# Two tiles of the first layer norm transposed by one DMA instead of two, and the transposed tiles laid out tile by tile

## The chip, the core and the metric

The kernel runs on one core of a Trainium2 chip. The time is the device time of one execution in microseconds; three executions of the kernel before gave 169.84, 170.46 and 170.59 us, so its median is 170.46 us. One more execution was profiled; its own time is 170.56 us, and the profile's times count from its first instruction.

Engines are named as in the profile: PE (TensorE matmuls), PEld (TensorE weight loads), DVE (VectorE), ACT (ScalarE), POOL (GpSimd) and SP (SyncE). SP computes nothing here: it issues all DMAs.

## The reference

A transformer block: linear attention on the layer norm of x, and a ReLU network on the layer norm of the result, each with a residual sum. The shapes are S = 2048 rows, D = 512, H = 32 heads of 16, Dff = 1792; everything is bfloat16.

```python
def _A_ref(x, wqkv, wo):
    q, k, v = ...                      # x @ wqkv, split into 32 heads of 16
    pq, pk = phi(q), phi(k)            # phi(t) = where(t > 0, t + 1, exp(t)) + 1e-6
    kv = einsum("bhsd,bhse->bhde", pk, v)
    z = einsum("bhsd->bhd", pk)
    num = einsum("bhqd,bhde->bhqe", pq, kv)
    den = einsum("bhqd,bhd->bhq", pq, z)[..., None] + 1e-6
    return (num / den) ... @ wo

h = x + _A_ref(_layernorm(x), A_wqkv, A_wo)
h2 = h + relu(_layernorm(h) @ w1) @ w2
```

## The kernel before

The 2048 rows are 16 tiles of 128 rows (tile number t, 0 to 15), and four tiles make a chunk of 512 rows (chunk c, 0 to 3). The order of all work is written out by hand in the string `ORDER`: each word names an operation and its numbers, and the words are carried out in that order. Engines run side by side; each engine takes its own instructions in the order of the words. So a word stands for a place in the queue of one engine.

The words that matter here, for a tile t of the first layer norm:

- `S.t` and `A.t` (DVE, L237 and L238) take mean and variance of x; `R.t.n` (ACT, L243 and L244) makes the reciprocal standard deviation of n tiles; `N.t` (DVE, L262) writes the normalised tile into `h_nat`.
- `X.t` (SP, L302) issues a transposing DMA that turns the tile of `h_nat` (128 rows by 512 features) into four blocks of 128 features by 128 rows, in `lnT[c]`. Tiles 0 to 3 go through PE instead (`T.t`, L281) and are copied from PSUM by ACT (`E.t`, L291).
- `K.t.b` (PE, L310) multiplies the transposed tile with the key weights: four matmuls of 512 columns into PSUM bank b, with the blocks of `lnT` as the stationary operand. `F`, `U` (ACT, L328 and L331), `M`, `D` (DVE, L335 and L338) make phi of the result.
- `G.t` (PE, L362) adds the tile's share of the sum over rows of layer norm times pk: four matmuls of 512 columns.
- `Q.c.j.b` (PE, L318) makes the queries of a whole chunk: four matmuls whose moving operand is `lnT[c]`, 512 rows wide.

After the attention, `lnT[c]` is used again for the second layer norm: `x.t` (SP, L303) transposes a tile of it by DMA, and `p.c.f.b` (PE, L521) multiplies a chunk with the first weights of the ReLU network, again with `lnT[c]` as the moving operand; `f` (PE, L541) is the second layer of that network, `fo` (DVE, L549) the last sum, and `fd` (SP, L556) the store.

Chunk 2 holds tiles 8 to 11. Its tiles are transposed in the order 9, 8, 11, 10. In `ORDER`, `N.9` is followed by `S.12`, `X.6`, `N.8`, `X.9`; `X.8` comes a line later. On PE the words stand as `K.7.3 G.1 K.6.2 K.9.1 G.4 K.8.0 G.5 G.6`.

The layout of a transposed chunk and how a tile is found in it:

```python
lnT = [big.tile([P, KD, CW], BF16, name=f"lnT{c}") for c in range(NCH)]   # KD = 4, CW = 512

def lnT_of(t, k=0, n=KD):
    c, j = divmod(t, CT)
    return lnT[c][:, k : k + n, j * P : (j + 1) * P]
```

So each partition of `lnT[c]` holds four feature blocks of 512 rows, and a tile's 128 rows lie in four pieces, one in each block.

Of the kernel before, what the change touches and what calls it, by code (L numbers as in the profile page):

```python
# [11 lines left out]
BF16 = mybir.dt.bfloat16  # L12
# [7 lines left out]
lx.4.2 A.2 T.0.7 E.0 warm.1.3 S.3 R.2.1 K.0.1.0.2 lx.6.2 A.3 R.3.1 K.0.1.2.2 N.1 T.1.5 F.0.1 E.1 N.2 N.3 T.3.2  # L20
lx.8.4 E.3 S.4 S.5 A.4 T.2.5 lx.12.4 lq.0.2 A.5 K.1.0.0.2 R.4.2 S.6 M.0.1 N.5 S.7 N.4 X.5 E.2 U.0.1 D.0.1 K.3.7
K.1.0.2.2 F.3.1 M.3.1 X.4 K.2.3.0.2 U.3.1 A.7 A.6 K.2.3.2.2 U.1.1 R.6.2 F.2.1 F.1.1 G.0 D.3.1 G.3 S.9 U.2.1 N.7
N.6 S.8 K.5.1 K.4.0 M.2.1 A.8 A.9 R.8.2 U.4.2 M.1.1 X.7 D.2.1 F.4.2 D.1.1 N.9 S.12 X.6 N.8 X.9 G.2 K.7.3 S.13
A.12 A.13 G.1 R.12.2 K.6.2 K.9.1 M.4.2 S.10 F.6.2 N.12 D.4.2 S.11 A.10 U.6.2 X.8 M.6.2 N.13 G.4 X.12 K.8.0 A.11
R.10.2 S.14 D.6.2 G.5 G.6 X.13 N.10 N.11 S.15 F.8.2 M.8.2 X.11 A.15 U.8.2 A.14 D.8.2 R.14.2 G.7 za.2 za.4 K.12.0
G.9 K.13.1 N.15 N.14 X.10 lq.2.2 K.11.3 F.12.2 K.10.2 M.12.2 U.12.2 F.10.2 masks X.15 X.14 lv.0.2 lv.2.2 l1.0.2
U.10.2 za.6 D.12.2 M.10.2 G.8 za.8 D.10.2 Q.0.1.1 Q.0.0.0 qF.0.0.2 qU.0.0.2 za.10 G.12 K.14.2 K.15.3 Q.0.2.0
# [29 lines left out]
def kernel(  # L57
# [10 lines left out]
    nc = tc.nc  # L68
    P = 128
    xf = A_x.flatten_outer_dims()  # L70
    of = out.flatten_outer_dims()
    S, D = xf.shape
# [4 lines left out]
    CW = 512  # L77
    CT = CW // P
    NCH = S // CW
    KD = D // P  # L80
# [8 lines left out]
    big = ctx.enter_context(tc.tile_pool(name="big", bufs=1))  # L89
# [12 lines left out]
    wq_sb = const.tile([P, KD, D], BF16, name="wq_sb")  # L102
    wk_sb = const.tile([P, KD, D], BF16, name="wk_sb")
    wv_sb = const.tile([P, KD, D], BF16, name="wv_sb")
    wo_sb = const.tile([P, KD, D], BF16, name="wo_sb")
    w1_sb = const.tile([P, KD, FF], BF16, name="w1_sb")
# [8 lines left out]

    h_nat = big.tile([P, NT, D], BF16, name="h_nat")
    ln_nat = h_nat
    lnT = [big.tile([P, KD, CW], BF16, name=f"lnT{c}") for c in range(NCH)]
    pqT = [big.tile([P, KD, CW], BF16, name=f"pqT{c}") for c in range(NCH)]
    gT = big.tile([P, KD, D], BF16, name="gT")  # L120
    kvbd = big.tile([P, KD, P], BF16, name="kvbd")
# [23 lines left out]
    bk = psum.tile([P, 8, CW], F32, name="bk")  # L145
# [127 lines left out]

    def lnT_of(t, k=0, n=KD):
        c, j = divmod(t, CT)
        return lnT[c][:, k : k + n, j * P : (j + 1) * P]

    def transpose(src, b, k, n):
        tp = bank16(b, n)
# [10 lines left out]
    def op_E(t, k=0, n=KD):  # L290
        nc.scalar.activation(out=lnT_of(t, k, n), in_=at_bank["T", t, k], func=ACT.Copy)  # L291

    def op_V(t, k=0, n=KD):
        nc.vector.tensor_copy(out=lnT_of(t, k, n), in_=at_bank["T", t, k])

    def op_e(t):
        nc.scalar.activation(out=lnT_of(t), in_=at_bank["t", t, 0], func=ACT.Copy)
# [4 lines left out]
    op_X = lambda t: nc.sync.dma_start_transpose(out=lnT_of(t), in_=ln_nat[:, t, :])  # L302
    op_x = lambda t: nc.sync.dma_start_transpose(out=lnT_of(t), in_=hn[:, t % NQ, :])  # L303


    def op_K(t, b, k=0, n=KD):
        c, j = divmod(t, CT)
        at_bank["k", t] = b
        for kd in range(k, k + n):
            nc.tensor.matmul(  # L310
                bk[:, b, :], lhsT=lnT[c][:, kd, j * P : (j + 1) * P], rhs=wk_sb[:, kd, :],
                start=(kd == 0), stop=(kd == KD - 1),
            )

    def op_Q(c, j, b):
        at_bank["q", c * KD + j] = b
        for kd in range(KD):
            nc.tensor.matmul(  # L318
                bk[:, b, :], lhsT=wq_sb[:, kd, j * P : (j + 1) * P], rhs=lnT[c][:, kd, :],
                start=(kd == 0), stop=(kd == KD - 1),  # L320
            )

# [194 lines left out]
    def op_p(c, f, b, s=0, n=1):  # L517
        at_bank["p", c, f] = b
        cols = slice(s * CW // n, (s + 1) * CW // n)
        for kd in range(KD):  # L520
            nc.tensor.matmul(  # L521
                bk[:, b, cols], lhsT=w1_sb[:, kd, f * P : (f + 1) * P], rhs=lnT[c][:, kd, cols],
                start=(kd == 0), stop=(kd == KD - 1),
            )

# [66 lines left out]
```

## Time and profile before

| | |
|---|---|
| three runs | 169.84, 170.46, 170.59 us |
| the profiled execution's own time | 170.56 us |
| its span, first to last instruction | 168.8 us |
| PE busy | 163.1 us, 855 matmuls recorded |
| DVE busy | 104.4 us |
| ACT busy | 65.1 us |
| DMA, share of 16 engines | 35.5% |

Between the profiled execution's own time and its span lie 1.8 us that no row of the trace shows. The page of the profile gives busy times, the chain of work that ended last (each step followed back to what released it), and the groups of instructions with what ended the idle time before them. Further views: the timeline of one engine in a stretch, in which neighbouring instructions of one kind are merged ("x4" are four of them, and the microseconds are from the first start to the last end); the DMA view, which lists issues with their median time from issue to landing; and the table of stretches, whose columns are the length, then for each engine its busy time and number of instructions, the granted clock of TensorE (1.00 is full speed), the mean busy share of the 16 DMA engines and the rate in GB/s. Matmul records overlap: a matmul's row is its latency, so the time that each takes in a row of equal ones is read from the distance between starts. Some matmul records are missing from the trace.

### The profile page before, as it was taken

Reading aid. Unit: us, or ns where it says so; the run is one execution under the profiler, and the core shown is the slowest. Engines: PE = TensorE matmul, PEld = TensorE weight load, DVE = VectorE, ACT = ScalarE, POOL = GpSimd, SP = SyncE. Lnnn points to the kernel's source line nnn. Section 1 sums busy time; section 2 is a strip of 40 time slices with the busy share of each in tenths; the row PEclk is TensorE's granted clock in tenths of the full one; section 3 lists DMA queues with packets and bytes.
Section 4 is the critical chain, followed back from the end, with each engine's and each line's share of the span. In section 5 each row is a group of like instructions: output and inputs, shape, how many; then the busy total and the mean of one; then the engine's idle time right before and its main releaser. Section 6 shows DMA issues by size and latency. Waiting matters only on the chain.

```text
span 168.8 us, 2286 instructions
## 1 busy us (share of the span) xinstructions
PE 163.1 (97%) x855; PEld 78.0 (46%) x871; DVE 104.4 (62%) x205; ACT 65.1 (39%) x97; POOL 4.8 (3%) x21
## 2 busy tenths in 40 slices
PE   7989999999999999999999999999999999999993
PEld 5344344445644454444444444444444444444553
DVE  3899998997668999699819879215102432050251
ACT  3698775875879947432000003004320420400000
POOL 7400000000000000000000000000000000000000
PEclk9999999999999999999999999999999999999999
DMA  4975575689533353534130015500320000002023
GB/s 112 352 245 97 97 66 124 176 270 378 174 64 65 77 138 87 134 62 95 37 62 0 31 31 122 126 4 0 62 93 0 31 0 4 0 0 93 0 65 94
DMA packets 30491, 15.49 MB, mean 92 GB/s; under 512 B 23184, under 2 KB 29328, under 8 KB 30480
## 3 DMA queue, kind: packets, MB, share of 16 engines
q1 hardware_dynamic: 30480, 15.34, 35.5%
q8 instruction: 7, 0.11, 0.3%
q14 instruction: 4, 0.03, 0.1%
HBM read 7.86 MB, written 2.10 MB: 59 GB/s over the span
## 4 chain that ended last, share of the span: by engine, by line
PE 85%; DVE 7%; DMA 4%; issue 1%; SPq 0%
PE bk L541 29%; PE bk L521 28%; PE bk L505 8%; PE bk L318 8%; PE bk L362 6%; PE bk L310 4%; DVE st L237 3%; DMA x_nat<-in_A_x_dram 2%; DMA lnT<-h_nat 2%; DVE h_nat L262 2%; PE bk L459 1%; DVE eb L335 1%; PE bk L403 1%; PE bk L415 1%; SPq L201 0%
## 5 line engine op out<-in xcount | busy, mean ns | idle before, releaser
L541 PE MATMUL bk<-w_sb,at 128*128 128x512 bf16 (+2 forms) x247 | 50.1, 355 | 0.3
L521 PE MATMUL bk<-lnT,w_sb 128*128 128x512 bf16 x219 | 50.0, 379 | 0.3
L527 ACT ACTIVATE at<-bk 128x1024 bf16<-128x1024 f32 x14 | 14.2, 1023 | 57.4 <-PE bk L521 57.4
L541 PEld LDWEIGHTS <-at 128*128 128x128 bf16 x252 | 23.6, 98 | 25.4 <-ACT at L527 0.3
L549 DVE SCALAR_TENSOR_TENSOR gT<-bk,rstd,h_nat 128x512 bf16<-128x512 f32 (+2 forms) x18 | 12.2, 689 | 35.7 <-PE bk L541 35.6
L521 PEld LDWEIGHTS <-w_sb 128*128 128x128 bf16 x224 | 21.8, 98 | 25.8
L532 DVE TENSOR_SCALAR at<-bk 128x1024 bf16<-128x1024 f32 x14 | 17.1, 1218 | 12.8 <-PE bk L521 12.6
L328 ACT ACTIVATE eb<-bk 128x1024 bf16<-128x1024 f32 (+1 forms) x18 | 16.6, 928 | 6.6 <-PE bk L310 4.8
L310 PE MATMUL bk<-wk_sb,lnT 128*128 128x512 bf16 x63 | 15.3, 380 | 0.4 <-ACT lnT L291 0.3
L505 PE MATMUL bk<-m_sb,pqs 128*128 128x512 bf16 x63 | 15.4, 380 | 0.1
L318 PE MATMUL bk<-lnT,wq_sb 128*128 128x512 bf16 x61 | 15.1, 379 | 0.1
L362 PE MATMUL bk<-at,h_nat 128*128 128x512 bf16 x55 | 13.5, 379 | 0.1
L331 ACT ACTIVATE rb<-bk 128x1024 bf16<-128x1024 f32 (+1 forms) x14 | 12.5, 904 | 0.3 <-PE bk L310 0.3
L511 DVE TENSOR_TENSOR h_nat<-bk,x_nat 128x512 bf16<-128x512 f32 x16 | 10.5, 680 | 2.9 <-PE bk L505 2.9
L237 DVE BATCH_NORM_STATS2 st<-x_nat 128x6 f32<-128x512 bf16 x16 | 10.8, 680 | 2.4 <-DMA x_nat<-in_A_x_dram 2.4
L239 DVE BATCH_NORM_STATS2 st<-h_nat 128x6 f32<-128x512 bf16 x16 | 10.7, 683 | 0.1
L310 PEld LDWEIGHTS <-lnT 128*128 128x128 bf16 x64 | 6.0, 98 | 8.4 <-ACT lnT L291 1.0
L362 PEld LDWEIGHTS <-h_nat 128*128 128x128 bf16 x64 | 6.2, 98 | 7.4 <-issue 0.2
L505 PEld LDWEIGHTS <-pqs 128*128 128x128 bf16 x64 | 5.9, 98 | 7.9 <-DVE pqs L495 1.8
L318 PEld LDWEIGHTS <-wq_sb 128*128 128x128 bf16 x64 | 5.9, 98 | 6.4
L472 ACT ACTIVATE wk_sb<-ld 128x1024 bf16<-128x1024 f32 x8 | 8.1, 1050 | 0.1
L335 DVE TENSOR_SCALAR eb<-eb 128x1024 bf16<-128x1024 bf16 (+1 forms) x18 | 6.8, 383 | 0.9 <-ACT eb L328 0.9
(63 smaller groups left out, 93.5 us busy)
## 6 DMA issues: line engine op xcount, KB each, us to landing
out_dram<-gT SPq DMA_DIRECT2D x15, 128.0 KB, 1.9
w_sb<-in_B_w_dram SPq DMA_DIRECT2D x2, 896.0 KB, 9.8
x_nat<-in_A_x_dram SPq DMA_DIRECT2D x2, 512.0 KB, 6.3
w_sb<-in_B_w_dram SPq DMA_DIRECT2D x2, 512.0 KB, 9.5
x_nat<-in_A_x_dram SPq DMA_DIRECT2D x3, 256.0 KB, 4.6
w_sb<-in_B_w_dram SPq DMA_DIRECT2D x2, 384.0 KB, 3.5
wk_sb<-in_A_wqkv_dram SPq DMA_DIRECT2D x2, 256.0 KB, 4.3
wq_sb<-in_A_wqkv_dram SPq DMA_DIRECT2D x2, 256.0 KB, 4.9
```

What stands on the lines that cost most here:

```text
L237: op_S = lambda t: nc.vector.bn_stats(out=st[:, t, :], in_=x_nat[:, t, :])
L310: nc.tensor.matmul(bk[:, b, :], lhsT=lnT[c][:, kd, j * P : (j + 1) * P], rhs=wk_sb[:, kd, :], start=(kd == 0), stop=(kd == KD - 1),)
L318: nc.tensor.matmul(bk[:, b, :], lhsT=wq_sb[:, kd, j * P : (j + 1) * P], rhs=lnT[c][:, kd, :], start=(kd == 0), stop=(kd == KD - 1),)
L328: nc.scalar.activation(out=buf(eb, kind, i, n), in_=bank(at_bank[kind, i], n), func=ACT.Exp)
L331: nc.scalar.activation(out=buf(rb, kind, i, n), in_=bank(at_bank[kind, i], n), func=ACT.Relu)
L362: nc.tensor.matmul(bk[:, KD + kd, :], lhsT=ln_nat[:, t, kd * P : (kd + 1) * P], rhs=pk(t)[:, 0, :], start=(t == 0), stop=(t == NT - 1),)
L505: nc.tensor.matmul(bk[:, b, :], lhsT=pqs[:, (c * KD + jb) % NQ, j * P : (j + 1) * P], rhs=m_sb[:, jb, :], start=(jb == 0), stop=(jb == KD ...
L521: nc.tensor.matmul(bk[:, b, cols], lhsT=w1_sb[:, kd, f * P : (f + 1) * P], rhs=lnT[c][:, kd, cols], start=(kd == 0), stop=(kd == KD - 1),)
L527: nc.scalar.activation(out=acts[c % 2][:, f : f + n, :], in_=bank(at_bank["p", c, f], n), func=ACT.Relu)
L532: nc.vector.tensor_scalar(out=acts[c % 2][:, f : f + n, :], in0=bank(at_bank["p", c, f], n), scalar1=0.0, scalar2=None, op0=ALU.max,)
L541: nc.tensor.matmul(bk[:, b, 0 : w * P], lhsT=acts[c % 2][:, f, j * P : (j + 1) * P], rhs=w2_sb[:, f, k * P : (k + w) * P], start=(f == 0), ...
L549: nc.vector.scalar_tensor_tensor(out=o_t[:, t % NO, cols], in0=bk[:, at_bank["f", t, k], 0 : w * P], scalar=rstd2[:, t : t + 1], in1=h_nat ...
```

## The change

Three things change.

1. `lnT[c]` is laid out tile by tile: first the tile in the chunk, then its feature block, then 128 rows. A tile's four blocks now lie side by side (512 elements of a partition). The four feature blocks of one tile are next to each other, and the 512 rows of one feature block, which the moving operand of `Q` and `p` reads, lie in four pieces of 128, 512 elements apart.
2. A new operation `XX.t` issues one transposing DMA for tiles t and t + 1: 128 rows by 1024 columns in, eight blocks out. `XX.8` stands where `X.9` stood, and `X.8` is gone.
3. `N.8` moves ahead of `S.12` and `X.6`, directly behind `N.9`.

```diff
-N.6 S.8 K.5.1 K.4.0 M.2.1 A.8 A.9 R.8.2 U.4.2 M.1.1 X.7 D.2.1 F.4.2 D.1.1 N.9 S.12 X.6 N.8 X.9 G.2 K.7.3 S.13
-A.12 A.13 G.1 R.12.2 K.6.2 K.9.1 M.4.2 S.10 F.6.2 N.12 D.4.2 S.11 A.10 U.6.2 X.8 M.6.2 N.13 G.4 X.12 K.8.0 A.11
+N.6 S.8 K.5.1 K.4.0 M.2.1 A.8 A.9 R.8.2 U.4.2 M.1.1 X.7 D.2.1 F.4.2 D.1.1 N.9 N.8 S.12 X.6 XX.8 G.2 K.7.3 S.13
+A.12 A.13 G.1 R.12.2 K.6.2 K.9.1 M.4.2 S.10 F.6.2 N.12 D.4.2 S.11 A.10 U.6.2 M.6.2 N.13 G.4 X.12 K.8.0 A.11
...
-    lnT = [big.tile([P, KD, CW], BF16, name=f"lnT{c}") for c in range(NCH)]
+    lnT = [big.tile([P, CT, KD, P], BF16, name=f"lnT{c}") for c in range(NCH)]
...
-        return lnT[c][:, k : k + n, j * P : (j + 1) * P]
+        return lnT[c][:, j, k : k + n, :]
...
+    def op_XX(t):
+        c, j = divmod(t, CT)
+        nc.sync.dma_start_transpose(
+            out=lnT[c][:, j : j + 2].rearrange("p t k n -> p (t k) n"),
+            in_=ln_nat[:, t : t + 2, :].rearrange("p t d -> p (t d)"),
+        )
...
-                bk[:, b, :], lhsT=lnT[c][:, kd, j * P : (j + 1) * P], rhs=wk_sb[:, kd, :],
+                bk[:, b, :], lhsT=lnT[c][:, j, kd, :], rhs=wk_sb[:, kd, :],
...
-                bk[:, b, :], lhsT=wq_sb[:, kd, j * P : (j + 1) * P], rhs=lnT[c][:, kd, :],
+                bk[:, b, :], lhsT=wq_sb[:, kd, j * P : (j + 1) * P], rhs=lnT[c][:, :, kd, :],
...
-                bk[:, b, cols], lhsT=w1_sb[:, kd, f * P : (f + 1) * P], rhs=lnT[c][:, kd, cols],
+                bk[:, b, cols], lhsT=w1_sb[:, kd, f * P : (f + 1) * P], rhs=lnT[c][:, s * CT // n : (s + 1) * CT // n, kd, :],
```

How the order of instructions moves, at two places. First DVE, around the normalising of tiles 9 and 8 (`h_nat` is where the normalised tiles go, `st` the statistics; the first L262 below is tile 9, the second tile 8, and the two L237 are the statistics of tiles 12 and 13). Before:

```order
L338 TENSOR_TENSOR at_94<-rb,eb 128x512
L338 TENSOR_TENSOR pk_lo<-rb,eb 128x512
L262 TENSOR_SCALAR h_nat<-x_nat,mv,rstd 128x512
L237 BN_STATS st<-x_nat 128x6
L262 TENSOR_SCALAR h_nat<-x_nat,mv,rstd 128x512
L237 BN_STATS st<-x_nat 128x6
L238 BN_AGGR mv<-st 128x2 x2
```

And with the change:

```order
L345 TENSOR_TENSOR at_94<-rb,eb 128x512
L345 TENSOR_TENSOR pk_lo<-rb,eb 128x512
L262 TENSOR_SCALAR h_nat<-x_nat,mv,rstd 128x512 x2
L237 BN_STATS st<-x_nat 128x6 x2
L238 BN_AGGR mv<-st 128x2 x2
```

Tile 8 is normalised directly behind tile 9, one statistics instruction earlier than before; that statistics instruction is one normalisation later, and from the second one on the order is as it was.

Second SP's queue of DMAs, from the first load of the query weights to the second (`lnT_82`, `lnT_83` and `lnT_84` are the chunks 1, 2 and 3). Before:

```order
L204 DMA wq_sb<-in_A_wqkv_dram 128x2x512
L302 DMA_TRANSPOSE lnT_82<-h_nat 128x4x128 x4
L302 DMA_TRANSPOSE lnT_83<-h_nat 128x4x128 x2
L302 DMA_TRANSPOSE lnT_84<-h_nat 128x4x128 x2
L302 DMA_TRANSPOSE lnT_83<-h_nat 128x4x128 x2
L204 DMA wq_sb<-in_A_wqkv_dram 128x2x512
```

And with the change:

```order
L204 DMA wq_sb<-in_A_wqkv_dram 128x2x512
L302 DMA_TRANSPOSE lnT_82<-h_nat 128x4x128 x4
L307 DMA_TRANSPOSE lnT_83<-h_nat 128x8x128
L302 DMA_TRANSPOSE lnT_84<-h_nat 128x4x128 x2
L302 DMA_TRANSPOSE lnT_83<-h_nat 128x4x128 x2
L204 DMA wq_sb<-in_A_wqkv_dram 128x2x512
```

The fifth and sixth transposing DMA, of tiles 9 and 8, are one; all others keep their place and size. PE's instructions keep their order.

## The prediction

> **What bounds the kernel now.** I read the page's shares first, then the chain of work that ended last, then the stretch around tiles 8 and 9.
>
> ```profile
> PE 163.1 (97%) x855; PEld 78.0 (46%) x871; DVE 104.4 (62%) x205; ACT 65.1 (39%) x97; POOL 4.8 (3%) x21
> PE 85%; DVE 7%; DMA 4%; issue 1%; SPq 0%
> ```
>
> PE is busy 97% of the span. The chain of waits (start, length, what) says from when on it alone sets the end:
>
> ```profile
> 16.77 0.31 DVE h_nat L262
> 17.09 0.57 DVE st L237
> 17.65 3.40 DMA lnT<-h_nat
> 21.05 0.04 issue
> 21.10 1.04 PE bk L310 x4
> 22.14 2.59 PE bk L362 x12
> ...
> 166.16 0.03 issue
> 166.18 0.35 DVE gT L549
> ```
>
> From 21.10 to 166.16 every step of the chain is PE or a gap of some 0.05 us. The step before is a transposing DMA of 3.40 us, issued at 17.65: that of tile 8, for which `K.8` waits. So what the change does to the moment at which PE gets through `K.8` goes to the end nearly in full, both ways. Changes on DVE, ACT or SP count only through this.
>
> The stretch itself, from the timelines of SP, PE, PEld and DVE:
>
> ```profile
> 15.04 1.22 SPq L302 DMA_TRANSPOSE lnT<-h_nat  x1
> 16.34 1.22 SPq L302 DMA_TRANSPOSE lnT<-h_nat  x1
> 17.65 1.22 SPq L302 DMA_TRANSPOSE lnT<-h_nat  x1
> 19.16 1.19 SPq L302 DMA_TRANSPOSE lnT<-h_nat  x1
> 18.21 1.89 PE L310 MATMUL bk<-wk_sb,lnT 128*128 128x512 bf16 x8
> 19.94 1.03 PE L362 MATMUL bk<-at,h_nat 128*128 128x512 bf16 x4
> 21.09 0.55 PEld L310 LDWEIGHTS <-lnT 128*128 128x128 bf16 x4 [0.63 <-DMA lnT<-h_nat]
> 15.76 0.41 DVE L262 TENSOR_SCALAR h_nat<-x_nat,mv,rstd 128x512 bf16<-128x512 bf16 x1
> 16.09 0.69 DVE L237 BATCH_NORM_STATS2 st<-x_nat 128x6 f32<-128x512 bf16 x1
> 16.69 0.40 DVE L262 TENSOR_SCALAR h_nat<-x_nat,mv,rstd 128x512 bf16<-128x512 bf16 x1
> 18.74 0.40 DVE L262 TENSOR_SCALAR h_nat<-x_nat,mv,rstd 128x512 bf16<-128x512 bf16 x1
> ```
>
> The SP rows are `X.6`, `X.9`, `X.8` and `X.12`. The eight matmuls from 18.21 are `K.6` and `K.9`. Eight take 1.73 us from start to start (19.94 − 18.21), 0.216 each, so `K.9` starts at 19.07. The four of `G.4` end their turn at 19.94 + 0.86 = 20.80. `K.8` starts at 21.10: PE stands still for 0.30 us there. `K.9` did not wait; `X.9` landed in time.
>
> Why `X.8` took 3.40 us, where others take 2.5:
>
> ```profile
> DMA to landing us min/median/max: 2.4/2.5/4.1
> q14 instruction: 1, 0.01, 8.5%
> ```
>
> The second row is the DMA view of the stretch 19.4 to 19.8: one instruction fetch lay on the DMA engines just as this transfer ended. That is an inference from the coincidence; it explains the extra 0.9 us.
>
> **The change part by part.**
>
> *The pair's issue.* `N.9` ends at 15.76 + 0.41 = 16.17. `N.8` now follows it instead of the statistics. Neighbouring normalisation and statistics start 0.33 apart (15.76 to 16.09), so `N.8` ends at 16.50. SP is through with `X.6` at 16.26. `X.12` was issued 0.02 behind its normalisation (18.74 + 0.40, then 19.16). So `XX.8` is issued at 16.5, against 16.34 for `X.9` and 17.65 for `X.8`.
>
> *Its landing* is the term that decides, and no row shows a transposing DMA of this size. What one tile's transfer consists of is seen in stretches of DMA activity:
>
> ```profile
> 17.40:17.60 0.20, 0.20 (x3) 0.08 (x2) 0.20 (x1) 0.20 (x1) 0.00 (x0) 1.00 0.14 23
> 17.60:18.20 0.60, 0.60 (x4) 0.26 (x3) 0.60 (x5) 0.42 (x2) 0.00 (x0) 1.00 1.02 202
> 18.20:18.40 0.20, 0.20 (x2) 0.10 (x1) 0.20 (x2) 0.17 (x2) 0.00 (x0) 1.00 0.19 28
> 18.40:18.80 0.40, 0.40 (x3) 0.20 (x2) 0.40 (x2) 0.07 (x1) 0.00 (x0) 1.00 0.00 0
> ```
>
> `X.9`, issued at 16.34, moves its data from about 17.55 to 18.3: 1.2 us until the data start, 0.75 us of data with the DMA engines full (share 1.02), and 0.5 us until the landing, 2.45 in all. Bounds for twice the data:
>
> - Low: it lands like one tile, after 2.4 us (the least landing time), at 18.9. `K.9` does not wait, and `K.8` finds its data there: PE gains the 0.30 us.
> - High: the issue doubles to 2.45, data begin only at its end, as they now begin when the issue of 1.22 ends, and take 1.5, then the 0.5: 4.45 us, at 20.95. `K.9` starts at 20.99, 1.92 late; less the 0.30 that `K.8` no longer waits, PE loses 1.62.
> - By the distance of two issues (17.65 − 16.34 = 1.31) instead of the data: 2.45 + 1.31 = 3.76, at 20.26, PE loses 20.30 − 19.07 − 0.30 = 0.93.
> - By the data alone: 2.45 + 0.75 = 3.2, at 19.7, PE loses 0.37.
>
> Which is nearest? A plain store of 128 KB:
>
> ```profile
> 92.54 0.36 SPq L556 DMA_DIRECT2D out_dram<-gT  x1
> 92.90:93.30 0.40, 0.40 (x4) 0.20 (x2) 0.28 (x1) 0.00 (x0) 0.00 (x0) 1.00 0.00 0
> 93.30:93.50 0.20, 0.20 (x3) 0.10 (x1) 0.00 (x0) 0.00 (x0) 0.00 (x0) 1.00 0.33 108
> ```
>
> Its issue ends at 92.90 and its data start after 93.30, at least 0.4 behind. A transposing DMA's data start when its issue ends, so they seem to stem from an early part of the issue, and a longer issue would overlap its data. I take the data bound with a little for the issue: 3.25 us, landing at 16.5 + 3.25 = 19.75.
>
> [...]
>
> *PE.* `K.9` starts at 19.79 (0.04 behind the landing, as after 21.05) in place of 19.07: +0.72. `G.4` follows at once, and `K.8`, whose tile lies in the same DMA, does not wait: −0.30. Sum **+0.42 us**. Queued behind the waiting `K.9` on PE are `G.4`, `K.8` and everything else, so the loss stays; DVE and ACT, which wait for `K.8`'s sums, only wait longer.
>
> *What is moved past.* The statistics of tile 12 start 0.33 later, those of tile 13 as before, so `N.12` (18.74) and `X.12` (19.16) stay; SP is free before: 16.5 + 2.45 at most is 18.95. One issue of about 1.2 is saved if the pair costs no more than one, on a queue that no later chain step shows: 0.
>
> *The layout.* ACT's copies into `lnT` wrote four pieces of 128 and now write 512 in a row; the rows show no cost of pieces to get back, since a copy into a plain row takes as long:
>
> ```profile
> L291 ACT ACTIVATE lnT<-bk x4: 579/594/604, 6.3 to 10.2; 128x512 bf16<-128x512 bf16 x4
> 14.01 0.60 ACT L331 ACTIVATE rb<-bk 128x512 bf16<-128x512 f32 x1
> ```
>
> The other transposing DMAs write contiguous rows now; PE waits for two of L302 at most (1.0 us of weight loads in all), of L303 never. So 0, while that cover holds. `K`'s weight loads still read 128 neighbours. But 64 matmuls of `Q` and 224 of `p` now read the moving operand in four pieces. No matmul of before does. Below: nothing. Above: each piece costs what a matmul of 128 columns costs by itself:
>
> ```profile
> 42.79 0.89 PE bk L403 x16
> 29.91 1.73 PE bk L318 x8
> ```
>
> 0.89 / 16 = 55.6 ns, times four 222.5, against 1.73 / 8 = 216.3 ns: 6.2 ns on 288 matmuls, 1.8 us. I take 0: a matmul of 512 columns already streams for 216 ns without a break that depends on where its columns lie, and the separate matmuls pay for a start of their own, which one instruction has not.
>
> Sum: 170.56 + 0.42 = 170.98 for the profiled execution, which lies 0.10 above the median of the runs: **170.9 us** against 170.46.
>
> **The rivals.**
>
> 1. *The pair lands like one tile* (low bound): PE gains 0.30, 170.2 us. For it: the granularity of an issue could be the instruction. Against it: the DMA engines are full (share 1.02) during one tile's 0.75 us, so twice the data needs more time, unless the contiguous destination moves faster. [...]
> 2. *The pair lands 4 us or more after its issue*, since data wait for the whole issue, or since they meet the fetch at 19.5, which cost `X.8` 0.9 us: 3.25 + 0.9 puts the landing at 20.65, PE loses 1.32; with the high bound 1.62. 171.8 to 172.1 us. For it: the fetch came at 19.5 and may come again, as DVE, ACT and SP reach that moment unchanged. Against it: the pair's data run from 17.7 to 19.2, just ahead. It decides as soon as the landing passes 20.2 (over 0.85 lost).
> 3. *The moving operand in pieces costs time*: 1.8 us on top of 0.42, 172.7 us; from 1.5 ns a matmul (0.43 us) on it carries the sum past 0.5%. For it: no row excludes it. Against it: above.
>
> **How the numbers follow.** Forecast 0.53, rival 1 0.07, rival 2 0.25, rival 3 0.12, and 0.03 for a gain that I cannot name. A measurement of this kernel tells about 0.5%, 0.85 us, from no change: 169.6 to 171.3. The forecast's own range is 170.6 to 171.3 (landing after 3.0 to 3.7 us); I give a tenth of it to beyond 171.3. Slower: 0.25 + 0.12 + 0.05 = 0.42. Faster: 0.03, since rival 1 gains only 0.2%. Within: 0.55. The range reaches from rival 1 to rival 2, 170.1 to 172.2; rival 3 and the unnamed gain stay out.
>
> **What would show it.** In the profile after: the issue of `XX.8` at 16.5 and its length (about 2 us if it grows with tiles), a landing 3.25 us behind, a wait of `K.9`'s weight load for a DMA on `lnT` ending at 19.8, none for `K.8`, and the chain entering PE there. The start-to-start of `Q` and `p` must stay at 216 ns; if it rises, rival 3 holds. A landing after 20.2 makes rival 2. Wrong in the other direction would be a chain in which `K.9` waits for nothing.

## The result and the profile after

The changed kernel takes 170.64 us, the median of 22 runs (170.23 to 171.36), against 170.38 us of 22 runs of the kernel before (169.58 to 170.82). The ratio is 1.0022, 95% interval 1.0011 to 1.0032: 0.2 to 0.55 us slower, a loss clear of zero in these runs but less than the 0.5% that the prediction took as the least a measurement tells from no change. The forecast was 170.9 us with 0.42 us lost.

The chain of waits of the changed kernel, where it enters PE:

```profile
16.32 3.13 DMA lnT<-h_nat
...
19.50 1.04 PE bk L317 x4
20.54 0.86 PE bk L369 x4
21.40 0.86 PE bk L317 x4
```

The transposing DMA is still the last thing ahead of PE, but it is now the pair's, and it holds up `K.9` (the first L317 row) and not `K.8` (the second). The same in the timelines of SP, PEld and PE (its first row below is `K.6`):

```profile
16.32 1.23 SPq L307 DMA_TRANSPOSE lnT<-h_nat  x1
15.23 0.75 PEld L369 LDWEIGHTS <-h_nat 128*128 128x128 bf16 x4
19.50 0.55 PEld L317 LDWEIGHTS <-lnT 128*128 128x128 bf16 x4 [0.93 <-DMA lnT<-h_nat]
20.16 0.75 PEld L369 LDWEIGHTS <-h_nat 128*128 128x128 bf16 x4
21.02 0.74 PEld L317 LDWEIGHTS <-lnT 128*128 128x128 bf16 x4
21.89 0.75 PEld L369 LDWEIGHTS <-h_nat 128*128 128x128 bf16 x4
18.03 1.03 PE L317 MATMUL bk<-wk_sb,lnT 128*128 128x512 bf16 x4
19.50 1.04 PE L317 MATMUL bk<-wk_sb,lnT 128*128 128x512 bf16 x4 [0.44 <-DMA lnT<-h_nat]
```

The issue takes 1.23 us, no more than that of one tile (1.22). `K.9` waits, and `K.8` at 21.02 has no wait behind its row. The table of stretches shows what the pair's DMA does meanwhile:

```profile
17.40:17.60 0.20, 0.20 (x3) 0.08 (x1) 0.20 (x3) 0.18 (x1) 0.00 (x0) 1.00 0.29 52
17.60:18.60 1.00, 1.00 (x6) 0.49 (x5) 1.00 (x4) 0.50 (x2) 0.00 (x0) 1.00 1.14 211
18.60:18.80 0.20, 0.20 (x3) 0.00 (x0) 0.20 (x2) 0.00 (x0) 0.00 (x0) 1.00 0.92 175
```

Data start 1.2 us after the issue, as with one tile, run for 1.4 us at 211 GB/s (one tile: 0.75 us at 202), and the landing follows at 19.45.

**A measure of the stage alone.** One profile against another can't be compared by its end: this one has a span of 168.5 us, less than the 168.8 of before, though the medians say the opposite. Two things that have nothing to do with the change differ. PE runs 0.18 us earlier already at `G.2` (15.23 against 15.41), after a first load of x that landed 0.2 us earlier (the chains have it at 1.72 + 3.66 against 1.71 + 3.87), and the later waits for `pqs` differ. Before, and after:

```profile
PEld L505 <- DVE pqs L495: 1.8, 4, 0.5
```

```profile
PEld L512 <- DVE pqs L502: 0.4, 2, 0.2
```

A second profile of the same changed kernel has 1.5 us there. So I compare a distance inside the stage: from the first weight load of `G.2` to that of `G.5`, between which lie `K.7`, `G.1`, `K.6`, `K.9`, `G.4` and `K.8`. Before, these two rows of PEld bound it (the first four loads of the second are `G.5`'s):

```profile
15.41 0.74 PEld L362 LDWEIGHTS <-h_nat 128*128 128x128 bf16 x4
21.76 1.18 PEld L362 LDWEIGHTS <-h_nat 128*128 128x128 bf16 x6
```

That is 6.35 us before and 21.89 − 15.23 = 6.66 after: +0.31. The four profiles without the pair lie within 0.03 us of each other in this distance (table below), so it tells differences of a tenth; those with the pair spread more, as its landing varies.

### The profile page after: what moved, and what is told of

Read it like the earlier page. It is cut to its first block, busy times and chain, and to the rows that moved or that the text cites. A ratio compares the mean times of both kernels' runs of the same rounds, so it can differ in the third digit from the quotient of the medians.

```text
span 168.5 us, 2286 instructions
## 1 busy us (share of the span) xinstructions
PE 162.2 (96%) x857; PEld 78.1 (46%) x871; DVE 104.5 (62%) x205; ACT 64.8 (38%) x97; POOL 4.7 (3%) x21
## 4 chain that ended last, share of the span: by engine, by line
PE 86%; DVE 6%; DMA 4%; issue 1%; SPq 0%
PE bk L528 29%; PE bk L548 29%; PE bk L325 8%; PE bk L512 8%; PE bk L369 6%; PE bk L317 4%; DVE st L237 3%; DMA x_nat<-in_A_x_dram 2%; DMA lnT<-h_nat 2%; DVE h_nat L262 1%; PE bk L466 1%; DVE eb L342 1%; PE bk L410 1%; SPq L201 0%; DVE mv L238 0%
## 5 line engine op out<-in xcount | busy, mean ns | idle before, releaser
L528 PE MATMUL bk<-lnT,w_sb 128*128 128x512 bf16 x224 | 50.5, 379 | 0.0
L528 PEld LDWEIGHTS <-w_sb 128*128 128x128 bf16 x224 | 21.8, 98 | 25.8
L317 PE MATMUL bk<-wk_sb,lnT 128*128 128x512 bf16 x63 | 15.5, 379 | 1.0 <-ACT lnT L291 0.5
L325 PE MATMUL bk<-lnT,wq_sb 128*128 128x512 bf16 x64 | 15.8, 379 | 0.1
L512 PE MATMUL bk<-m_sb,pqs 128*128 128x512 bf16 x61 | 14.8, 379 | 0.1
L237 DVE BATCH_NORM_STATS2 st<-x_nat 128x6 f32<-128x512 bf16 x16 | 10.7, 681 | 2.2 <-DMA x_nat<-in_A_x_dram 2.2
L317 PEld LDWEIGHTS <-lnT 128*128 128x128 bf16 x64 | 6.0, 98 | 8.7 <-DMA lnT<-h_nat 1.3
L325 PEld LDWEIGHTS <-wq_sb 128*128 128x128 bf16 x64 | 5.9, 97 | 6.4
```

The lines of the kernel that those rows point to most:

```text
L237: op_S = lambda t: nc.vector.bn_stats(out=st[:, t, :], in_=x_nat[:, t, :])
L317: nc.tensor.matmul(bk[:, b, :], lhsT=lnT[c][:, j, kd, :], rhs=wk_sb[:, kd, :], start=(kd == 0), stop=(kd == KD - 1),)
L325: nc.tensor.matmul(bk[:, b, :], lhsT=wq_sb[:, kd, j * P : (j + 1) * P], rhs=lnT[c][:, :, kd, :], start=(kd == 0), stop=(kd == KD - 1),)
L512: nc.tensor.matmul(bk[:, b, :], lhsT=pqs[:, (c * KD + jb) % NQ, j * P : (j + 1) * P], rhs=m_sb[:, jb, :], start=(jb == 0), stop=(jb == KD ...
L528: nc.tensor.matmul(bk[:, b, cols], lhsT=w1_sb[:, kd, f * P : (f + 1) * P], rhs=lnT[c][:, s * CT // n : (s + 1) * CT // n, kd, :], start=(k ...
```

## The experiments

Each is a change to the changed kernel, except the third, which is one to the kernel before. "Stage" is the distance just described; ratios are against the kernel before.

| | stage, us | against 6.35 | ratio, 95% interval |
|---|---|---|---|
| e1, layout only | 6.37 | +0.02 | 1.0012, 0.9991 to 1.0033 |
| e2, two DMAs, N.8 early | 6.38 | +0.03 | 1.0008, 0.9987 to 1.0029 |
| e6, other pairs | 6.38 | +0.03 | 0.9997, 0.998 to 1.0014 |
| e5, pair issued earlier | 6.43 | +0.08 | 0.9994, 0.9972 to 1.0017 |
| e8, the change again | 6.56 | +0.21 | 1.0006, 0.9987 to 1.0026 |
| the change, first profile | 6.66 | +0.31 | 1.0022, 1.0011 to 1.0032 |
| e4, e10, the change with DMAs added much later | 6.77, 6.83 | +0.42, +0.48 | one run each |
| e7, two pairs | 6.75 | +0.40 | 1.0028, 1.0008 to 1.0047 |
| e9, pair issued later | 8.43 | +2.08 | 1.013, 1.0098 to 1.0162 |

### e1: the layout alone

```diff
 (changed kernel)
-ORDER of the change
+ORDER of the kernel before
```

> The new layout of lnT with the order of before: tiles 9 and 8 by two DMAs, N.8 where it was. My theory: the layout costs nothing, the time is that of before within 0.1% (ratio 1.000), and the start-to-start time of the matmuls of Q and p stays at 216 ns. Rival (moving operand read in pieces): 6 ns on each of 288 matmuls, 1.8 us, ratio 1.010. If the rise of 0.2% of the whole change came from the layout, ratio 1.002.

The chain of waits of e1:

```profile
17.41 3.42 DMA lnT<-h_nat
...
29.69 1.73 PE bk L325 x8
...
124.11 3.45 PE bk L528 x16
```

Eight matmuls of `Q` (L325) take 1.73 us and sixteen of `p` (L528) 3.45, both with the moving operand in four pieces; the kernel before has the same numbers in its chain with the operand in one run:

```profile
53.41 1.73 PE bk L318 x8
...
113.41 3.45 PE bk L521 x16
```

So pieces of 128 columns cost nothing that these rows show, and `K.8` waits as in the kernel before. The timing agrees but is wide: its interval reaches to +0.3%.

### e2: everything but the merging

```diff
-... D.1.1 N.9 N.8 S.12 X.6 XX.8 G.2 ...
+... D.1.1 N.9 N.8 S.12 X.6 X.9 X.8 G.2 ...
```

> The whole change but for the merging: new layout, N.8 directly behind N.9, then X.9 and X.8 as two DMAs one behind the other. My theory: X.8 is still held by the issue of X.9 (1.2 us), lands where it landed in before, K.9 does not wait, so the time is that of before within 0.1%, and 0.2% below that of the whole change. Rival (the earlier N.8, which pushes the statistics of tile 12 back, is what costs): ratio 1.002 as with the whole change.

```profile
17.78 3.45 DMA lnT<-h_nat
15.56 0.53 PEld L369 LDWEIGHTS <-h_nat 128*128 128x128 bf16 x3
21.94 0.74 PEld L369 LDWEIGHTS <-h_nat 128*128 128x128 bf16 x4
```

The first row is from the chain of waits, the other two, `G.2` and `G.5`, from the timeline of PEld. `X.8` is again issued 1.3 us behind `X.9` and lands 3.45 us later; the earlier `N.8` buys and costs nothing (+0.03 in the stage). What remains between e2 and the whole change is the merging alone: 6.56 to 6.83 in its four profiles against 6.38. The timings alone would not have told the two apart.

### e3: other work for PE ahead of `K.8` (kernel before)

```diff
-... G.4 X.12 K.8.0 A.11 R.10.2 S.14 D.6.2 G.5 G.6 ...
+... G.4 X.12 G.5 K.8.0 A.11 R.10.2 S.14 D.6.2 G.6 ...
```

> The kernel before, with the four matmuls G.5 moved ahead of K.8 on PE, so that PE has work while the transpose of tile 8 lands. My theory: the 0.30 us that PE stands still ahead of K.8 go to the end in full, ratio 0.998, K.8 without a wait. Rival (a later wait, such as that for pqs at 50 us and 72 us, takes a gain or a loss of this size up): ratio 1.000, with the weight loads of L505 waiting longer.

A miss: ratio 1.0009, 0.9988 to 1.003, where 0.998 was expected. `G.6`, which follows in both orders, starts 22.84 − 22.38 = 0.46 earlier (timelines of PE), of which 0.15 is an earlier start of the whole stage (15.41 against 15.26 at `G.2`); so the 0.31 was gained. But it is lost two steps on. Timelines of PE and ACT:

```profile
22.58 1.02 ACT L328 ACTIVATE eb<-bk 128x1024 bf16<-128x1024 f32 x1 [0.99 <-PE bk L310]
23.50 1.02 ACT L331 ACTIVATE rb<-bk 128x1024 bf16<-128x1024 f32 x1
24.57 1.02 PE L310 MATMUL bk<-wk_sb,lnT 128*128 128x512 bf16 x4 [0.30 <-ACT rb L331]
```

`K.12` writes the PSUM bank that `K.8` used, and ACT reads that bank until 24.52. With `K.8` moved back behind `G.5`, ACT starts on it at 22.58 in place of 22.17, and `K.12` waits. It starts 24.57 − 15.26 = 9.31 us behind `G.2`, against 24.56 − 15.41 = 9.15 before: a little more was lost than gained. Neither theory had this: the wait moved, not to 50 us but to the next user of the bank.

### e4 and e10: one DMA of 1, 2 and 4 tiles

```diff
+    def op_y(n):
+        dst = {1: wo_sb, 2: wv_sb, 4: wq_sb}[n]
+        nc.sync.dma_start_transpose(
+            out=dst[:, 0:n, :].rearrange("p k (b n) -> p (k b) n", n=P),
+            in_=x_nat[:, 0:n, :].rearrange("p t d -> p (t d)"),
+        )
...
-... hD.13 fo.3 x.5 p.1.0.6 ...
+... hD.13 fo.3 x.5 y.2 y.1 y.4 p.1.0.6 ...
```

> The changed kernel with three transposing DMAs more, of 2, 1 and 4 tiles of x into weights that are no longer needed, issued from about 86 us on, where SP and the DMA engines are idle; they do work that nobody reads. My theory (one issue of fixed length, then data at one rate): issues of about 1.2 us whatever the size; landings 2.45, 3.15 and 4.55 us after the issue for 1, 2 and 4 tiles, 0.7 us for each tile more. [...] The time stays that of the changed kernel.

Issues on SP and, from the DMA view, the times to landing:

```profile
86.93 1.28 SPq L315 DMA_TRANSPOSE wv_sb<-x_nat  x1
88.32 1.22 SPq L315 DMA_TRANSPOSE wo_sb<-x_nat  x1
89.63 2.11 SPq L315 DMA_TRANSPOSE wq_sb<-x_nat  x1
...
wv_sb<-x_nat SPq DMA_TRANSPOSE x1, 3.2
wo_sb<-x_nat SPq DMA_TRANSPOSE x1, 2.4
wq_sb<-x_nat SPq DMA_TRANSPOSE x1, 4.3
```

The landings are 2.4, 3.2 and 4.3 us for 1, 2 and 4 tiles: 0.55 to 0.8 us for each tile more. The issue hardly differs between one tile and two (1.22 and 1.28 us), as in the theory; that of four tiles took 2.11, against its 1.2. The next run asked whether that came from the DMAs ahead of it (`y.4 y.2 y.1` in place of `y.2 y.1 y.4`):

> The run with three sizes again, with the DMA of 4 tiles issued first, on an idle queue. If the 2.1 us issue of the 4 tiles came from what stood ahead of it, the issue is 1.2 to 1.3 us now; if it comes from the size, 2.1 us again. Landing 4.3 to 4.6 us behind the issue in both cases, since the data move at one rate of some 0.7 us a tile. The DMAs of 2 tiles and of 1 behind it land later than 3.2 and 2.4, since they queue behind its data.

```profile
87.61 1.81 SPq L315 DMA_TRANSPOSE wq_sb<-x_nat  x1
89.48 1.85 SPq L315 DMA_TRANSPOSE wv_sb<-x_nat  x1
...
wq_sb<-x_nat SPq DMA_TRANSPOSE x1, 4.4
```

Inconclusive: 1.81 us for the four, between the two expectations, and the queue was not idle, as a transpose of the kernel's own was issued just ahead. Two tiles behind the four took 1.85 where they took 1.28 before. So what is under way ahead of it seems to matter for the issue; whether size does too is open, the more so as a single tile's issue reaches 1.68 us elsewhere in the changed kernel (the longest of L302). The landing of four tiles, 4.4, came as expected; the two tiles queued behind them landed after 3.9.

### e5, e7, e8: the pair earlier, two pairs, and the change again

e5 moves the two normalisations ahead of a DVE step, so that the pair can be issued earlier:

```diff
-... D.2.1 F.4.2 D.1.1 N.9 N.8 S.12 X.6 XX.8 ...
+... D.2.1 F.4.2 N.9 N.8 D.1.1 S.12 X.6 XX.8 ...
```

> The whole change, with N.9 and N.8 moved ahead of D.1.1 on DVE, so that the pair's DMA can be issued some 0.2 us earlier (SP is free behind X.6 by then). My theory: the wait of K.9 is what the change costs, and it ends a fixed 3.15 us behind the issue; it shrinks by 0.2 us, so PE comes out of K.8 0.15 to 0.25 us behind where it was in the kernel before, in place of 0.3 to 0.45, and the ratio is 1.001. Rival (the DMA's length does not set it): the wait stays at 0.6 to 0.7 us.

```profile
16.19 1.24 SPq L307 DMA_TRANSPOSE lnT<-h_nat  x1
19.29 0.55 PEld L317 LDWEIGHTS <-lnT 128*128 128x128 bf16 x4 [0.70 <-DMA lnT<-h_nat]
```

The landing is 3.06 us behind the issue (3.13 in the change), the wait of `K.9` falls from 0.93 to 0.70, and the stage from +0.31 to +0.08, better than expected. Part of that is a short landing: e8 below has one as short (3.04 us by its chain, 3.06 here) without the earlier issue and is at +0.21, so the earlier issue itself gave 0.13. With the `K.8` gain in hand, this version is where the kernel before is: ratio 0.9994, 0.9972 to 1.0017.

e7 merges tiles 7 and 6 too (`X.7` goes, `X.6` becomes `XX.6`):

```diff
-... M.1.1 X.7 D.2.1 F.4.2 D.1.1 N.9 N.8 S.12 X.6 XX.8 ...
+... M.1.1 D.2.1 F.4.2 D.1.1 N.9 N.8 S.12 XX.6 XX.8 ...
```

> The whole change, with tiles 7 and 6 merged too. My theory: K.7 waits 0.8 us for its pair (issue at 14.05, landing at 17.2, K.7 was at 16.5); K.9, now 0.8 us later, finds its tile there and does not wait, and neither does K.8: 0.5 us in all, hardly more than with one pair, ratio 1.003. Rival (each merging costs its own 0.4 us or more, and they add): 1.1 us, ratio 1.0065.

```profile
17.34 0.33 PEld L317 LDWEIGHTS <-lnT 128*128 128x128 bf16 x3 [1.02 <-DMA lnT<-h_nat]
19.86 0.61 PEld L317 LDWEIGHTS <-lnT 128*128 128x128 bf16 x4 [0.25 <-DMA lnT<-h_nat]
```

`K.7` now waits 1.02 us and `K.9` only 0.25. The waits cover each other: +0.40 in all, ratio 1.0028, where a sum of two would have been 1.0065. The forecast of 0.5 was a little high.

e8 is the changed kernel once more.

> The changed kernel itself, beside the three others of this call. My theory: ratio 1.002, K.9 waits 0.6 to 0.7 us, K.8 not at all, PE comes out of K.8 0.3 to 0.45 us behind the kernel before. If the layout had a cost, it would show as a further distance that grows through the matmuls of Q and p.

```profile
16.61 1.23 SPq L307 DMA_TRANSPOSE lnT<-h_nat  x1
19.69 0.55 PEld L317 LDWEIGHTS <-lnT 128*128 128x128 bf16 x4 [0.84 <-DMA lnT<-h_nat]
```

`K.9` starts 3.08 us behind the issue, the stage is at +0.21, a little under what was expected, and the ratio of these 12 runs, 1.0006, has an interval that holds both 1.000 and 1.002.

### e6: pairs where nothing waits

```diff
 (new layout, ORDER of the kernel before)
-... M.8.2 X.11 A.15 ... X.10 lq.2.2 ... X.15 X.14 ...
+... M.8.2 XX.10 A.15 ... lq.2.2 ... XX.14 ...
```

> New layout, tiles 9 and 8 by two DMAs as before, but tiles 11 and 10, and 15 and 14, by one DMA each. My theory: a merged DMA lands 3.15 us behind its issue, at about 26.2 and 31.1, and the matmuls that read them start later than that (K.11 at 26.9), so nothing waits, ratio 1.000. Rival (merging itself costs, wherever it is): PE loses 0.3 us or more at K.11 and at K.14, ratio 1.004.

The view of L307 in e6, where it issues these two pairs:

```profile
L307 SPq DMA_TRANSPOSE lnT<-h_nat x2: 1238/1343/1448, 23.2 to 28.1; - x2
...
who waited for it (us, times):
busy tenths in 40 slices 0000000000000000000000000000000000000000
DMA to landing us min/median/max: 3.1/3.2/3.4
```

Nobody waited for either, though both took 3.1 us and more; ratio 0.9997, 0.998 to 1.0014. In these runs merging cost time where the first reader stood ready, and only there.

### e9: the pair later

```diff
-... S.12 X.6 XX.8 G.2 ...
+... S.12 X.6 y.1 XX.8 G.2 ...
```

> The whole change with one transposing DMA more ahead of the pair's in SP's queue (a tile of x into weights not yet loaded, read by nobody), so that the pair is issued 1.1 to 1.3 us later, at about 17.65. My theory (a wait of K.9 goes to the end in full): the pair lands at 20.9, K.9 starts 1.9 us later than in the kernel before, and PE comes out of K.8 1.6 us behind, ratio 1.008 to 1.0095, the lower one if the waits for pqs at 50 and 72 us take up to 0.25 us of it. If the instruction fetch at 19.5 meets its data, 0.9 us more, ratio 1.013 to 1.015. Rival (DVE and ACT have slack that catches PE up later): the distance shrinks to under half by the end, ratio 1.004 or less.

`y.1` is the DMA of one tile from e4. The chain of waits, and PEld:

```profile
17.34 3.77 DMA lnT<-h_nat
...
21.15 0.55 PEld L324 LDWEIGHTS <-lnT 128*128 128x128 bf16 x4 [2.71 <-DMA lnT<-h_nat]
```

The landing came 3.77 us behind the issue, and an instruction fetch fell among its data (the DMA view of 19 to 19.6 has the row `q14 instruction: 1, 0.01, 3.2%`). The stage is at +2.08, between the 1.6 expected without a fetch and the 2.5 (0.9 more) with one. The time is at 1.013, 1.0098 to 1.0162, that is 1.7 to 2.8 us; the medians, 172.10 and 170.20, differ by 1.9. So the loss goes to the end in full or nearly, and the rival with slack on DVE and ACT (1.004) is out. This holds for the size of the change as well, as far as the mechanism is the same.

## Why the prediction was right

- **The issue at 16.5.** It came at 16.32 in a profile whose PE runs 0.18 earlier: 16.5. The gate was `N.8`, as forecast; where e5 moves `N.8` forward, the issue follows.
- **The landing after 3.25 us.** 3.13 in the change, 3.04 to 3.30 for the same pair in e4, e5, e7, e8 and e10, 3.2 for the two tiles that e4 adds. The choice between 2.4 and 4.45 rested on the full DMA engines (share 1.02), and that was the right row: the data took 1.4 us in place of 0.75, and the rest of the DMA stayed (1.2 us until the data, 0.55 from their end to the landing, against 1.2 and 0.5). The small addition for a longer issue was not needed: the issue stayed at 1.23. The about 2 us that the prediction names for one that grows with the tiles was an estimate, which this pair did not show.
- **The wait of `K.9`, +0.72, less 0.30 for `K.8`.** From the start of `K.6` to that of `K.9` it is 0.86 before and 19.50 − 18.03 = 1.47 after, so +0.61; `K.8` has no wait, so −0.30. The net, 0.31 here, is 0.21 to 0.48 in the four profiles that have this stage; the 0.42 lies among them.
- **That it goes to the end.** Shown with a larger delay by e9; for the 0.3 us of the change itself it is supported but not shown. Its medians, +0.26 us by difference and 0.2 to 0.55 by the ratio, fit, but the interval of e8, the same kernel again, also allows no loss at all. From `G.2` to the end of the span the profiles overlap: 152.9 to 153.4 us without the pair (before, e1, e2, e6), 153.3 to 153.6 with it (the change, e4, e8, e10), 155.0 in e9.
- **The layout at nothing.** Shown by e1: the same 1.73 us for eight matmuls. Rival 3 is out. That separate matmuls pay for a start of their own was my reading of 55.6 against 216.3 / 4 = 54.1 ns; no run isolates it.
- **Rival 1**, the landing of a single tile, is out: 3.13 us against 2.45. The condition under which it would have held, a contiguous destination that moves faster, was not shown: 211 GB/s against 202, 1.4 us of data against 0.75.
- **Rival 2**, a landing beyond 20.2, did not come, but it was near, and that it did not come was in part luck. The prediction had the fetch at 19.5, 0.3 us behind the end of the data; in the profile of the change it began at 18.94, within 0.05 us of the pair's last data (DMA view of 18.7 to 19.2), and the landing came at 19.45, 3.13 us behind the issue. In e9, with the pair about 1 us later, it fell among the data, and the landing took 3.77.
- **That `X.8` was late because of the fetch** stays an inference, but a better one than the prediction had. `X.8` landed 3.40 to 3.45 us behind its issue in the four profiles whose chain shows it (the kernel before 3.40, e1 3.42, e2 and e6 3.45), where the median is 2.5, so it is no accident of one profile. Its data were not slow: in the kernel before they were through by about 19.65, 2.0 us behind the issue like those of `X.9`, and then the engines stood nearly idle (share 0.02), but the landing came only at 21.05. The table of stretches, before:

```profile
19.60:20.00 0.40, 0.40 (x4) 0.17 (x3) 0.40 (x2) 0.40 (x1) 0.00 (x0) 1.00 0.02 1
```

  In the kernel before the fetch begins at 19.53 (DMA view of 19.4 to 19.8), 1.88 us behind the issue, while the last data are still moving, and the landing follows its beginning by 1.52 us. In the profile of the change it began only after the last of the pair's data. No run moved the fetch itself; e9 moved a pair into it, and the landing took 3.77 in place of 3.04 to 3.30.

## What to carry to other kernels

Merging two DMAs delayed the first half to the landing of the whole: 3.13 us behind the issue in place of 2.45, with 1.4 us of data in place of 0.75. Count that against whoever reads the first half, by the data time of the second half. The issue saved (1.22 us on SP) gained nothing visible here: `K.9` waited for the landing. Where the readers came late (e6: 3.1 to 3.4 us to the landing, nobody waited), merging cost nothing that the runs show.

A stall ahead of one matmul group is not always free time to be filled: here moving work into the 0.30 us delayed the next user of the same PSUM bank, which started 9.31 in place of 9.15 us behind `G.2`, and gave back the gain (e3).

For differences of 0.2%, a distance between two instructions of the stage tells more than the whole time, as the rest of the kernel adds waits that vary by several tenths of a microsecond from one profile to the next (here those for `pqs`: 1.8 us before, 0.4 and 1.5 in two profiles of the change).

## What the runs showed of the hardware

- A transposing DMA of one and of two tiles of 128 by 512 bf16 took the same issue, 1.2 us, in most rows (medians of one tile 1.208 and 1.210 before and after; the pair 1.23), and landed after 2.5 us (the median of one tile) and 3.0 to 3.4 us (two tiles; 3.77 in e9 with a fetch among the data, 3.9 in e10 behind the DMA of four tiles). Longer issues occur for one tile (1.68 in the changed kernel) and for two (1.45 in e6, 1.85 in e10). Four tiles landed after 4.3 us (e4) and 4.4 (e10), with issues of 2.11 and 1.81 us whose cause is open.
- A matmul whose 512 moving columns lie in four pieces of 128, 1 KB apart, took the same 216 ns (1.73 us for eight and 3.45 for sixteen in e1) as one with a single run (1.73 and 3.45 in the kernel before).
- Instruction fetches show up on the DMA engines, and transposing DMAs with one beside them landed up to 1.8 us after the median of 2.5; that the fetch is the cause is an inference. In the changed kernel the longest landing of L302 is 4.3 us, that of `X.12`, beside a fetch at about 21.2:

```profile
q8 instruction: 1, 0.02, 5.8%
```

That row is of the stretch 20.6 to 21.6. Nothing waited for that tile. A fetch does not always come with a late landing: the pair's, with one right behind its data, came after 3.13 us.
